# The same 1286 items of a gated delta-rule plus softplus MLP kernel, issued in another order

## The chip, the core and the metric

One core of one Trainium2 chip. The metric is device time in microseconds (us) of one execution; lower is better. Three runs of the kernel before took 242.27, 242.74 and 242.04 us: a median of 242.27.

The engines are named as the profile names them: PE (matrix multiply) with PEld (its weight loads), DVE (vector), ACT (scalar), POOL (GpSimd) and SP (the queue that issues most transfers). Each takes its own instructions strictly in order; between engines only semaphores order the work.

## What is computed

```python
# q, k, v, g: [4, 8, 768, 48]; beta: [4, 8, 768]; w_in: [384, 2048]; w_out: [2048, 384]
k_n = k / (np.linalg.norm(k, axis=-1, keepdims=True) + 1e-06)
state = zeros((B, H, D, D))
for t in range(S):
    y[:, :, t] = g[:, :, t] * (q[:, :, t] @ state)
    v_old = state^T @ k_n[:, :, t]
    state = state + beta[:, :, t] * outer(k_n[:, :, t], v[:, :, t] - v_old)
x = y.transpose(0, 2, 1, 3).reshape(3072, 384)
out = softplus(x @ w_in) @ w_out
```

The loop is written here in short form; sums run over the 48 features of a head.

## The kernel before, in words

The 768 steps are cut into 12 chunks of 64. The chunks are taken in six pairs (0 and 1, 2 and 3, and so on). All the work is recorded first, as 1286 items, each a small function that emits a few instructions and knows which items it depends on. Then `Program.emit` walks the words of the table `_ORDER`. A word is a letter and a number: `G281` emits item 281 on POOL; P is PE, D is DVE, A is ACT, S is SP. The table alone sets the order on every engine and, where an item may run on more than one engine, which one. It also sets which buffer an item gets: each ring of buffers gives the one that came free first at that place of the table, and an item waits until the last user of its buffer is done.

Some items matter below. The stages of a chunk c are:

- `load`: k, q, v and g come in two halves of 192 KB each, issued by SP (L302 for q, L305 for the others). Items 25 + 8c and 26 + 8c are k, the next two q, then v, then g. `bload` (17 to 24) are eight small transfers of beta.
- `ksq`, `red`, `sqrt` or `pow`, `eps`: the norms of k. A square (L351 on ACT, L353 on POOL), a sum on DVE (L362), a root (ACT for chunks 0 to 3, L373 on POOL after that), a reciprocal (L383).
- `kmul` (L406) scales k by its norm for chunks 2 and up; chunks 0 and 1 are only cast. `cast q` makes q 16-bit. `trs` are transposes on PE (L422 for k, L454 for q), `kev` and `qev` copy them out of PSUM.
- `gram` (L516): products of k and q within the chunk. `kkc` (L209 or L213) copies, `mask` (L498) masks them.
- For each pair, the inverse of a triangular matrix: `ln` (L597 or L604), `pick` (L627), `clear`, `diag`, two `prep` (L644), then 15 `step` items in a strict chain, step 0 with one instruction (L656) and each later one with a multiply (L664) and an add (L671), on DVE or POOL. Then `ca` and `cb` (L686, L688), the stream transposes `st` (L714), `tx`, and three small product stages per chunk: `xmm`/`xs`, `tmm`/`td2`, `zmm`/`z`. The items of the first pair are 225 to 272 (steps 231 to 245), of the second 313 to 360 (steps 319 to 333).
- The recurrence of the chunk: `ks` and `qs` (L826) multiply by the state, `vs` (L842) and `w` (L866; `w0`, L858, in chunk 0) form the right side, `umm` (L880), `u1`, `zu` (L893), `u2` solve, `smm` (L910) and `s` (L924) give the next state, `ymm` (L936) and `y` (L950) the output, `ytr` (L963) and `xt` transpose it for the MLP. Chunk c + 1 needs `s` of chunk c.
- The MLP: `g1` (L989) multiplies by w_in, `soft` (L1001) is the softplus on ACT, `g2` (L1016) multiplies by w_out, `o` copies the result, `store` (L1035) writes it. Chunks 0, 1, 10 and 11 go alone, with a moving size of 256 in `g1`; chunks 2 and 3, 4 and 5, 6 and 7, 8 and 9 go in pairs with 512, so `g1 2.*` and `g1 4.*` begin a pair. `wload` (121 to 128, L330) are the eight weight transfers, issued by POOL: 121 to 124 the quarters of w_in, which are called w0.0 to w0.3, and 125 to 128 those of w_out.
- `fill` (L1046): four matmuls on the identity whose result nobody reads. They are optional: the table may hold any number of them.

PSUM has eight banks: five for the small stages (ring `d`), two for `g1` (ring `h`), one for `g2` (ring `o`). SBUF has 12 buffers for loaded k, q, v, g and for the squares of k (ring `f`).

What sets the order is thus the table alone. SP's list is a queue with loads and stores in one line: a store at its head waits for its `o`, and all loads behind it wait too. POOL's list mixes arithmetic with the weight transfers.

## Time and profile before

| | |
|---|---|
| median of 3 runs | 242.27 us (242.04 to 242.74) |
| span of the profiled execution | 241.5 us |
| PE busy | 219.4 us, 91% |
| of it, `g1` and `g2` | 74.0 and 77.7 us |
| of it, `fill` (13 items, 52 matmuls) | 18.1 us |
| DVE, ACT, POOL busy | 161.7, 152.8, 113.7 us |
| loads and weights, HBM read | 25.26 MB |

The span runs from the first to the last instruction of the profiled execution. Its own time outside the profiler isn't listed; the median of the runs is 0.8 us above its span.

How to read it: times are from the span's start. A busy share is an average over stages that have different limits. An idle engine costs nothing unless the engine that sets the end waits for it. Starts and ends of PE's matmuls overlap, since they are pipelined, and the spans on POOL are rough.

### The profile page before, as it was taken

How to read it: one execution, taken by the hardware profiler on the slowest of the kernel's cores; microseconds unless marked ns; L12 is line 12 of the kernel's file. 1: busy time of each engine (PE TensorE's matmuls, PEld its weight loads, DVE VectorE, ACT ScalarE, POOL GpSimd, SP SyncE). 2: the span in 40 equal slices, each digit the busy share in tenths (PEclk: the TensorE clock that was granted, in tenths of full speed). 3: DMA queues.
4: the chain of work that ended last, by engine and by line, in shares of the span. 5: the costliest groups of instructions: out<-in, count | busy, mean ns of one | idle time of the engine just before them, and what ended most of it. 6: DMA issues, size and time to landing. Idle time of an engine off the chain costs nothing.

```text
span 241.5 us, 11396 instructions
## 1 busy us (share of the span) xinstructions
PE 219.4 (91%) x5020; PEld 135.6 (56%) x5020; DVE 161.7 (67%) x368; ACT 152.8 (63%) x292; POOL 113.7 (47%) x197
## 2 busy tenths in 40 slices
PE   7645877879988999999999999999999999999983
PEld 2423455646764664556655566655565555677751
DVE  2768699888897889987899757896496310623000
ACT  5767576764982778876895767757363674143540
POOL 8740393875779778989597482016620000000000
PEclk9985599999999999999999999999999999999999
DMA  6999989999999399961889514962302311303112
GB/s 102 182 245 137 167 135 190 176 173 180 180 217 167 57 177 164 162 113 35 150 153 184 97 30 94 160 122 52 69 21 52 68 34 25 64 19 81 35 33 65
DMA packets 86833, 27.57 MB, mean 114 GB/s; under 512 B 77048, under 2 KB 86776, under 8 KB 86784
## 3 DMA queue, kind: packets, MB, share of 16 engines
q1 hardware_dynamic: 80624, 20.83, 52.6%
q0 software_dynamic: 3840, 3.17, 8.5%
q10 hardware_dynamic: 2320, 2.85, 5.2%
q8 instruction: 39, 0.64, 1.2%
q14 instruction: 10, 0.08, 0.1%
HBM read 25.26 MB, written 4.72 MB: 124 GB/s over the span
## 4 chain that ended last, share of the span: by engine, by line
PE 75%; DMA 7%; DVE 6%; SPq 4%; issue 3%; ACT 2%; POOL 1%; DVEq 0%; ACTq 0%; POOLq 0%
PE o L1016 27%; PE h L989 26%; DMA w_in<-in_moe_w_in_dram 4%; PE d L826 3%; SPq L305 3%; PE d L936 3%; PE d L516 2%; DMA f<-in_q_dram 2%; PE d L422 2%; PE d L963 2%; PE d L454 2%; PE d L880 2%; PE d L910 2%; PE d L893 2%; PE d L768 1%
## 5 line engine op out<-in xcount | busy, mean ns | idle before, releaser
L1016 PE MATMUL o<-w_out,ga 128*128 128x384 f16 x384 | 77.7, 327 | 0.7 <-ACT osb L209 0.6
L1001 ACT ACTIVATE ga<-h 128x512 f16<-128x512 f32 x96 | 56.5, 599 | 29.8 <-PE h L989 25.9
L989 PE MATMUL h<-xt,w_in 128*128 128x512 f16 (+1 forms) x384 | 74.0, 327 | 0.5 <-DMA w_in<-in_moe_w_in_dram 0.3
L989 PEld LDWEIGHTS <-w_in 128*128 128x128 f16 x384 | 34.5, 98 | 21.2 <-DMA w_in<-in_moe_w_in_dram 0.8
L1016 PEld LDWEIGHTS <-ga 128*128 128x128 f16 x384 | 33.7, 98 | 21.8 <-issue 0.8
L664 POOL TENSOR_TENSOR tmp<-nn,tt 128x78 f32<-128x78 f32 (+7 forms) x53 | 19.2, 362 | 16.1 <-DVE tt L671 13.0
L373 POOL TENSOR_TENSOR nv<-nv,half_c 128x16 f32<-128x16 f32 x8 | 23.5, 2940 | 6.6 <-DVE nv L362 6.5
L671 POOL TENSOR_TENSOR tt<-tt,tmp 128x78 f32<-128x78 f32 (+7 forms) x53 | 20.4, 385 | 4.2
L498 DVE TENSOR_TENSOR mt<-d,mask 128x256 f16<-128x256 f32 x48 | 18.2, 413 | 4.5 <-PE d L516 3.5
L209 ACT ACTIVATE kqt<-d 128x1024 f16<-128x1024 f16 (+1 forms) x18 | 18.0, 1000 | 4.8 <-PE d L454 3.6
L211 DVE CAST u<-d 128x384 f16<-128x384 f32 x20 | 10.9, 554 | 14.3 <-PE d L880 7.9
L209 ACT ACTIVATE u<-d 128x384 f16<-128x384 f32 x28 | 13.0, 490 | 11.8 <-PE d L880 5.4
L1046 PE MATMUL h<-ident 128*128 128x512 f16 x52 | 18.1, 493 | 1.7 <-DVE ident L197 1.7
L209 ACT ACTIVATE kk<-d 128x256 f16<-128x256 f32 x37 | 13.4, 386 | 6.3 <-PE d L516 5.4
L209 ACT ACTIVATE osb<-o 128x384 f32<-128x384 f32 x19 | 9.3, 492 | 9.4 <-PE o L1016 9.3
L454 PE MATMUL d<-ident,qn 128*128 128x128 f16 x96 | 8.5, 243 | 6.7 <-ACT qn L209 5.9
L950 DVE TENSOR_TENSOR yg<-d,f 128x384 f16<-128x384 f32 x24 | 12.3, 551 | 2.9 <-PE d L936 2.8
L924 DVE TENSOR_TENSOR s<-s,d 128x384 f16<-128x384 f16 x20 | 10.4, 542 | 5.7 <-PE d L910 4.3
L644 POOL TENSOR_TENSOR nn<-ln,beta_l 128x256 f32<-128x256 f16 x8 | 6.1, 780 | 14.2 <-DVE ln L627 14.2
L209 ACT ACTIVATE xt<-d 128x768 f16<-128x768 f16 x10 | 8.1, 813 | 7.0 <-PE d L963 7.0
L866 DVE TENSOR_TENSOR w<-f,d 128x384 f16<-128x384 f32 x22 | 11.3, 545 | 1.4 <-ACT xt L209 0.7
L362 DVE TENSOR_REDUCE nv<-f 128x16 f32<-128x768 f32 x12 | 11.3, 942 | 1.0 <-ACT f L351 1.0
(117 smaller groups left out, 346.7 us busy)
## 6 DMA issues: line engine op xcount, KB each, us to landing
f<-in_k_dram SPq DMA_DIRECT2D x24, 192.0 KB, 5.7
f<-in_q_dram SPq DMA_DIRECT2D x24, 192.0 KB, 5.6
f<-in_v_dram SPq DMA_DIRECT2D x24, 192.0 KB, 5.3
f<-in_g_dram SPq DMA_DIRECT2D x24, 192.0 KB, 5.3
out_dram<-osb ACTq DMA_DIRECT2D x29, 96.0 KB, 2.7
out_dram<-osb SPq DMA_DIRECT2D x19, 96.0 KB, 2.8
w_in<-in_moe_w_in_dram POOLq DMA_DIRECT2D x4, 384.0 KB, 7.9
w_out<-in_moe_w_out_dram POOLq DMA_DIRECT2D x4, 384.0 KB, 8.4
```

The costliest lines, as they stand in the source:

```text
L209: nc.scalar.activation(o, x, AF.Copy, scale=float(sign))
L362: lambda en: nc.vector.tensor_reduce(nvs().rearrange("p (a h) -> p a h", a=2), ksq.ap, mybir.AxisListType.X, ALU.add),
L373: nc.gpsimd.tensor_tensor(nvs(), nvs(), half_c[:, :NU], ALU.pow)
L454: nc.tensor.transpose(o[:, j], qn.ap[:, j].rearrange("p m d -> p (m d)"), ident)
L498: nc.vector.tensor_tensor(mt[c][m].ap[:, NP * p : NP * p + NP], gb[m].ap.rearrange("p (i b) -> p i b", i=NP)[:, :, n : n + C], mask[:, Non ...
L664: ENG[en].tensor_tensor(t, nn.ap[:, :, j : j + 1, j + 1 :].broadcast_to([P, 2, w, n]), tt.ap[:, :, :w, j : j + 1].broadcast_to([P, 2, w, n ...
L671: ENG[en].tensor_tensor(rows, rows, t, ALU.add)
L950: lambda en, m=m: nc.vector.tensor_tensor(heads(yg.ap, m), hd(yp[m].ap), heads(gf.ap, m), ALU.mult),
L989: nc.tensor.matmul(hp.ap[:, n * b : n * b + n], w_in[:, j, f * P : (f + 1) * P], xt.ap[:, j, t0 : t0 + n], start=(j == 0), stop=(j == 2),)
L1001: lambda en, hp=hp, o=gb: nc.scalar.activation(o.ap, hp.ap, AF.Softplus),
L1016: nc.tensor.matmul(op.ap[:, :DM], b.ap[:, col + c0 : col + c0 + 128], w_out[:, f, :], start=(f == 0), stop=(f == NF - 1),)
L1046: nc.tensor.matmul(hp.ap, ident, ident[:, None, :].broadcast_to([P, 4, P]))
```

## The change

Only the text of `_ORDER` is changed. Items, dependences, ring sizes and shapes are the same. Counted over the two tables:

- SP's loads. Before: k0, k1, q2, v0, half of k3, q1, q0, q4, q3, the rest of k3, half of g0, k2, k4, ... After: k0, k1, q1, q0, half of k3, k2 and k3 mixed with one half of q2, half of g0, q3, q4, v0, k4, the other half of q2, the rest of g0, v1, g1, ... The eight `bload` go from places 19 to 33 of SP's list to places 10 to 28. SP issues 27 of the 48 stores (19 before), ACT 21 (29 before).
- The first inverse: steps 3, 4, 5, 8, 9, 11, 12, 13 and 14 run on POOL, the others on DVE. Before, step 2 ran on POOL, the others on DVE. All 15-step chains together: 68 steps on POOL (58 before), 22 on DVE (32 before).
- The second inverse: its two `prep` and step 10 move from POOL to DVE, steps 2, 3, 5, 6, 7, 9 and 12 from DVE to POOL, so that step 10 is the only one left on DVE.
- POOL's list up to the second inverse. After: cast k0 (half), five copies, clear, clear, diag, cast q0, the nine steps, w0.3, w0.0, kmul 2, ksq 4, diag, cast q2, the two `w0` of chunk 0 (items 714 and 715), w0.1, kmul 3, pow 4, w0.2, two quarters of w_out, vs 1, kmul 4, two quarters of w_out, then the steps. Before: copies, cast k1 (half), cast q2, `w0` twice, diag, step 2, ksq 2, tx, w0.0, w0.2, w0.1, clear, ksq 4, two of w_out, diag, pow 4, kmul 4, w0.3, vs 1, the two `prep`, steps.
- `kmul` 2 and 3 move from DVE to POOL; six of the 12 `xt` move from ACT to DVE; single `cast`, `kev`, `kkc`, `td2`, `u1`, `u2`, `z`, `o` move in both directions.
- PE: 10 `fill` items (13 before). In chunk 2, `smm` stands before `ymm`, and `ks` of chunk 3 stands before `ytr` of chunk 2; before, `ymm` stood before `smm` and `ytr` 2 before `ks` 3. On DVE, `w` of chunk 3 stands before `ln` of the third pair (item 401); before, it stood behind it.
- Before the first `g1` of the pair of chunks 2 and 3 (item 992 before, 1000 after) PE's list holds the same items in both tables, but for the fills and for the last `g2` of chunk 1, which stands behind it after.

The tables up to the first `g1` of the pair of chunks 2 and 3; the rest is permuted in the same manner:

```diff
@@ -1064,72 +1064,72 @@
 _ORDER = """
-S26 S25 P138 P161 S33 S34 P151 A12 G4 S44 A173 S43 G2 A169 D176 P177 P174 D0 G227 A178 P188 D170 A15
-A3 S29 G1 D175 P182 A189 A171 D204 S30 S49 A190 A197 D183 P205 D206 S36 G201 A11 P158 S35 S28 D184
-G9 D198 P202 G280 D203 D172 P281 A199 D200 D225 P216 G714 P210 A211 A212 G715 D226 P141 A282 P185
-A187 A7 S27 S60 S59 S52 D5 P213 A217 A10 A207 S51 S50 A218 A179 P180 A214 A181 A186 G228 D229 D230
-S22 P208 A209 D231 D232 G233 D234 D235 D236 P133 S32 S24 A215 S41 D237 D238 D239 D240 D241 D242 D243
-D244 D245 D248 D246 A293 D250 S23 S42 G273 A368 P369 S57 A370 S66 P145 P194 P136 P255 A247 A249 S31
-S58 S17 D196 P264 D251 D195 S18 D257 A254 D256 G253 P258 A300 G8 D252 G121 D265 A260 P301 P135 G123
-D294 S20 D266 S19 D274 G6 A259 P261 P716 A13 A295 A262 A263 A717 A718 P191 D192 A275 S21 P719 A720
-S38 S37 D193 D302 D721 P147 A713 G122 D16 P219 S65 G315 G14 G361 G126 P725 D221 G125 D220 P722 D727
-D726 G316 P728 D296 P137 D276 D297 D277 A724 A723 A729 P934 P928 A935 A929 D362 G363 P298 D299 P926
-A927 S40 P278 D279 P303 A304 P308 A310 A309 P930 D306 D305 P283 A284 A285 P936 D307 D312 D364 P288
-A931 D311 G365 D287 D292 P731 P932 A289 A290 A937 S39 D291 D286 D313 G124 P366 P267 A268 A269 G730
-P150 P270 S67 S45 A933 D314 G317 G318 D733 A381 G319 G320 A367 D732 S46 D382 P735 A737 A736 D272
-D271 P949 P950 D321 D322 G127 G323 P222 D224 P734 S68 D223 D324 D325 S73 P738 P938 A739 A740 P744
-A939 D326 D745 P940 G327 P371 P741 D746 D328 P747 G128 P164 S81 D742 A748 G329 A372 S99 D743 A941
-G330 P951 D374 P970 A373 D331 P376 A388 P956 A971 G332 D379 D380 P749 D375 S74 G333 A378 D334 P958
-A377 A957 D751 G383 A959 D336 P964 D338 A337 P389 S82 A335 P962 A390 D339 G342 P952 A965 S48 P343
-D384 P352 S76 A341 D345 D344 G385 A953 D750 D340 P960 P346 A449 A348 S84 P942 A961 S47 A963 D347
-D354 P753 A754 P349 A469 S75 P966 D450 D351 G451 A350 D755 D353 P968 S83 A967 P386 D470 S100 S98
-D387 P752 P756 D758 P943 D757 G471 S53 D452 P391 A393 S54 P944 D392 A954 D395 P762 D394 D764 P396
-A397 A955 P759 D760 A398 P945 D761 A946 D401 S97 P355 P972 G403 G453 A356 A969 P454 G476 S55 A357
-P973 D763 A455 S56 P765 D402 G404 G405 D400 P974 A766 D399 G406 P767 A456 P358 D769 P975 G407 A360
-D768 G408 P457 D359 A976 A978 S977 P770 G409 D458 G410 P771 A772 P979 S105 D773 A557 P477 D411 P774
-G412 D775 A776 S62 P980 A564 D472 P780 S61 G413 A478 P777 D781 P981 D782 G414 A947 D473 P783 A784
-P459 P982 D460 D461 P992 A983 D462 D778 P474 S64 A993 P1008 D558 S92 A475 P1000 D779 A1009 P464 S89
-D463 P479 A1001 P986 D468 A481 S113 D482 A466 D483 P990 D480 G415 G491 G416 G417 G418 G419 A987 D465
...
+A2 S25 S26 G173 G7 P132 A4 P160 D176 G9 A169 S34 S33 G12 D170 P155 G1 S35 S36 S27 S28 S49 S23 D5 D6
+D13 A14 A201 G8 D204 A197 P174 P177 D3 D175 D0 D198 P205 P202 A206 A203 P210 A171 D172 A199 A211
+A212 A15 D200 D178 P182 D225 G315 G227 P130 D183 D184 D226 G228 D229 G179 D16 D230 S42 S44 D231 D232
+D233 S18 S41 S21 S50 S32 S22 P180 A181 P194 A273 D207 S51 S60 S17 S19 S29 S52 S58 S20 S59 S24 D195
+D274 D196 G234 S30 P208 P185 A209 G235 A187 A186 P188 P213 A214 P216 A217 A215 P219 D10 G236 D237
+D238 G239 P154 G240 D241 G242 G243 G244 G245 A275 A11 D190 D221 A293 D294 D220 S57 S43 P191 D193
+D192 S31 S37 D276 D248 A368 A249 A189 S38 S39 D246 S40 P135 D250 A295 A247 D296 P166 A218 S65 S66
+G124 G121 G277 G361 G316 P255 G280 G714 P369 A370 A713 D251 P264 P278 D300 D257 D253 D254 D256 P258
+G715 P157 A259 D252 G122 G297 S46 S45 A260 P261 A263 D266 D362 D265 G363 P716 S74 S73 A717 P168 P281
+A262 D718 G123 A279 P719 A721 A720 P301 P298 D302 P725 A299 A282 D727 D726 P153 P303 A304 S68 S67
+D305 D306 P728 P288 D307 D291 D403 A729 A289 P308 P283 G126 G125 G730 D364 D311 D312 D292 A290 A309
+P928 P722 G365 A310 A284 A285 D287 S82 S81 P267 A929 A724 A268 P932 D313 D314 D317 D318 A933 P222
+P938 P940 A723 A269 A939 P731 P926 A941 A927 D224 D223 D286 P366 P270 D733 D732 P936 P735 S48 A272
+D271 P734 P934 S47 A937 A737 D736 P738 A740 P930 G127 D367 P371 A372 A931 G128 D739 P744 D745 G319
+G320 G321 D746 P949 G322 G323 G324 G325 G326 G327 G328 D329 G330 G331 P747 P950 P741 D742 D743 S53
+A748 P956 A935 A957 G332 G333 S54 P376 P962 D374 A963 D379 D378 D380 D375 P958 P951 G381 P966 D337
+A373 A334 A335 P952 D336 D338 D404 P749 P343 A959 A953 A967 A377 D339 P942 G341 D345 D382 S75 D750
+P964 P943 P970 A971 G342 S76 D344 D340 P346 P352 A348 D751 D353 P944 A347 P349 P753 A449 D354 A351
+G383 D350 D384 G385 A754 A755 D388 P960 D450 D579 P752 P756 P389 D757 A961 P945 A758 P759 D946 A390
+A469 P386 D760 D761 D470 P762 P968 S56 S84 S83 A387 P391 P972 S55 G451 D452 D763 G453 G456 P396 A969
+A965 A393 A392 P973 D394 D395 D400 D399 A398 A397 D764 P767 P355 A356 A357 D768 G471 D769 S98 S97
+P454 P974 P771 A455 P358 A773 P765 P975 A359 A360 A772 A766 A976 P770 P774 D401 D402 D405 D406 D407
+D408 D409 D410 A776 A775 P457 P979 P780 A476 P777 D781 D782 D778 D779 P980 A458 P477 P783 A478 D784
+A557 P981 P459 D472 D473 P1000 P1012 P474 A1001 D461 D462 D463 A1013 P1008 P992 P464 A475 P479 A1009
+A993 P990 G411 G412 G413 G414 D415 D416 D417 G418 G419 G420 G421 P986 D468 A460 A466 D482 D481 D483
...
 """
```

81 lines of the change are left out of this document (41 added, 40 removed).

## The prediction

> **What bounds the kernel now.** First the page, then the windows, then the engines' timelines.
>
> ```profile
> span 241.5 us, 11396 instructions
> PE 219.4 (91%) x5020; PEld 135.6 (56%) x5020; DVE 161.7 (67%) x368; ACT 152.8 (63%) x292; POOL 113.7 (47%) x197
> PEclk9985599999999999999999999999999999999999
> DMA  6999989999999399961889514962302311303112
> ...
> L1046 PE MATMUL h<-ident 128*128 128x512 f16 x52 | 18.1, 493 | 1.7 <-DVE ident L197 1.7
> ```
>
> ```profile
> 0.00:18.00 18.00, 11.21 (x236) 5.79 (x236) 10.31 (x36) 11.62 (x25) 11.99 (x27) 0.97 1.04 176
> 18.00:30.00 12.00, 8.71 (x72) 4.42 (x76) 9.35 (x28) 8.03 (x13) 1.82 (x2) 0.50 1.09 155
> 0.00:90.00 90.00, 72.57 (x1846) 47.12 (x1847) 72.40 (x177) 60.18 (x118) 58.34 (x92) 0.92 1.03 166
> 90.00:238.00 148.00, 146.80 (x3176) 88.52 (x3174) 89.29 (x192) 92.54 (x175) 55.38 (x105) 1.00 0.47 84
> ```
>
> The columns after the length are PE, PEld, DVE, ACT, POOL, clock, DMA share, GB/s. Behind 90 us PE is busy 146.8 of 148 us: it sets the end there. Ahead of 90 us it is busy 72.57 us, of which 18.1 are fills, so 90 - 72.57 + 18.1 = 35.5 us bring the result no nearer. Only there can an order win much. What ends that part is the first 512-wide `g1`, which needs `xt` of chunk 3:
>
> ```profile
> 40.51 0.72 PE L989 MATMUL h<-xt,w_in 128*128 128x256 f16 x5 [0.34 <-DMA w_in<-in_moe_w_in_dram]
> ...
> 89.77 0.81 PE L989 MATMUL h<-xt,w_in 128*128 128x512 f16 x3
> ```
>
> The first row is the very first `g1`; the second is where the saturated part begins. From there to the end of the span it is 241.5 - 89.8 = 151.7 us, and PE has the same items left in both orders (one `g2` more in the new one, 0.7 us). So the sum is: the new time of that matmul, plus 151.7 + 0.7 = 152.4. The median is 0.8 us above the span, which I add at the end.
>
> Four marks lie on the way there: the first inverse's end, chunk 0's output, the second inverse, and the recurrence of chunks 2 and 3.
>
> **The loads.** In the first 18 us the transfers run at 176 GB/s (first window), so a half of 192 KB takes 1.1 us of the 16 engines, and the digits show them full until slice 13.
>
> ```profile
> 26.91 1.47 POOL L353 TENSOR_TENSOR f<-f 128x768 f32<-128x768 f32 x1 [9.52 <-DMA f<-in_k_dram]
> ...
> 31.69 8.77 DMA w_in<-in_moe_w_in_dram
> ```
>
> The first row is POOL's timeline: `ksq` 2 waits 9.5 us for k2, whose last half is the 21st load. In the new order it is the 12th: 9 x 1.1 = 10 us earlier, about 17 to 18 us; k3 follows at 19. The price is on the other side: v0 goes from the 8th to the 21st place, 13 x 1.1 + 5 more beta transfers, so it lands near 28 us instead of 13; the second half of q2 becomes the 23rd (near 32), k4 the 22nd (near 30).
>
> **The first inverse.** Nine steps go from DVE to POOL, one comes back.
>
> ```profile
> L671 POOL TENSOR_TENSOR tt<-tt,tmp 128x110 f32<-128x110 f32 x3 | 1.2, 407 | 0.2
> L664 POOL TENSOR_TENSOR tmp<-nn,tt 128x110 f32<-128x110 f32 x3 | 1.2, 393 | 0.7 <-DVE tt L671 0.6
> L671 DVE TENSOR_TENSOR tt<-tt,tmp 128x110 f32<-128x110 f32 x3 | 0.8, 273 | 0.1
> L664 DVE TENSOR_TENSOR tmp<-nn,tt 128x110 f32<-128x110 f32 x3 | 0.8, 271 | 0.1
> L362 DVE TENSOR_REDUCE nv<-f 128x16 f32<-128x768 f32 x7 | 6.6, 945 | 0.2 <-ACT f L351 0.2
> ...
> 16.29 0.22 DVE L671 TENSOR_TENSOR tt<-tt,tmp 128x56 f32<-128x56 f32 x1
> ...
> 16.65 0.32 POOL L664 TENSOR_TENSOR tmp<-nn,tt 128x78 f32<-128x78 f32 x1 [1.95 <-DVE tt L671]
> ```
>
> A step of this width is 0.80 us on POOL and 0.54 on DVE: 0.26 more, and a POOL instruction leaves a slightly longer gap (last column: 0.2 us before three, against 0.1). The nine are 30 to 126 wide; I take 0.28 for each, 2.5. A handover costs 0.14 (16.29 + 0.22 to 16.65), and there are five against two: 0.5. DVE is to do `red` 2 (0.95) and two masks between steps 2 and 6, of which some 0.5 us stick out beyond POOL's three steps; step 2, which returns, gives 0.3 back. Together +3.2. What the chain starts from stays where it was, since its inputs k0 and k1 are still loaded first.
>
> ```profile
> 24.59 0.78 DVE L688 TENSOR_SCALAR ta<-tt,mx 128x256 f16<-128x256 f32 x2
> ...
> 47.48 1.93 DVE L604 STREAM_TRANSPOSE ln<-kk 128x1024 uint32<-128x1024 uint32 x1
> ...
> 62.74 0.44 DVE L688 TENSOR_SCALAR ta<-tt,mx 128x256 f16<-128x256 f32 x1 [0.25 <-POOL tt L671]
> ...
> 78.05 1.96 DVE L604 STREAM_TRANSPOSE ln<-kk 128x1024 uint32<-128x1024 uint32 x1
> ```
>
> On DVE's timeline the first row is where the first inverse's result is taken; it moves from 24.6 to 27.8 us. The Trainium skill, GPSIMD Engine Reference, section 4.1, speaks against such a move: two-input elementwise work is to stay on VectorE, about 2x slower on GpSimd. The rows above say 1.5x; by the page the nine steps would cost some 5 us, and the result would be 242.5.
>
> **Chunk 0.** Behind the steps POOL has two weight issues (0.8 each), `kmul` 2, `ksq` 4, a diag, `cast q` 2 and both `w0`. The rows:
>
> ```profile
> L353 POOL TENSOR_TENSOR f<-f 128x768 f32<-128x768 f32 x3 | 4.4, 1468 | 9.5 <-DMA f<-in_k_dram 9.5
> L858 POOL TENSOR_TENSOR w<-f,nv 128x384 f16<-128x384 f32 x2 | 1.6, 834 | 1.3 <-DVE bl L582 1.3
> 46.07 1.47 POOL L406 TENSOR_TENSOR kn<-f,nv 128x768 f16<-128x768 f32 x1 [0.73 <-DVE nv L383]
> 33.67 0.44 PE L880 MATMUL d<-w,td 64*64 64x48 f16 x32 [0.25 <-DVE xs L753]
> ```
>
> 27.8 + 1.6 + 1.5 + 1.5 + 0.2 + 0.8 + 1.7 = 35.1, if k4 and q2 have landed by 31 and 32.6, which is just in time. So `umm` 0 starts at 35.4 instead of 33.7, and the first `g1` at about 42 instead of 40.5. This is not yet a loss of 1.5 us: PE has no lack of `g1` of chunks 0 and 1 to do later, while it waits for chunks 2 and 3.
>
> **The second inverse.** `kmul` 3 on POOL comes at 35.1 + 0.8 (w0.1) + 1.5 = 37.4, so the transposes of k3 at 38, four us ahead of before, and `ln` 2 about 43.3 instead of 47.5. But POOL has more in line: `pow` 4, three weight issues, `vs` 1, `kmul` 4, two weight issues.
>
> ```profile
> L373 POOL TENSOR_TENSOR nv<-nv,half_c 128x16 f32<-128x16 f32 x5 | 14.7, 2934 | 6.0 <-DVE nv L362 5.9
> 48.38 1.49 POOL L842 TENSOR_TENSOR f<-f,nv 128x768 f32<-128x768 f32 x1
> 51.75 0.24 POOL L656 TENSOR_TENSOR tt<-nn,tt 128x30 f32<-128x30 f32 x1
> ```
>
> 37.4 + 3.3 (with its add) + 5 x 0.8 + 1.5 + 1.5 = 47.7 for step 0, against 51.75. Seven steps more run on POOL and one fewer: 7 x 0.26 less 0.2 for the two that change places, so 12.6 us in place of 11.0. It ends at 60.3, 2.4 us ahead of 62.7.
>
> **Chunks 2 and 3.** From the inverse's end to the first 512-wide `g1` it takes 89.8 - 62.7 = 27.0 us before. Where it is lost:
>
> ```profile
> 69.06 0.44 PE L880 MATMUL d<-w,td 64*64 64x48 f16 x32 [0.50 <-DVE td L211]
> 73.02 0.35 PE L893 MATMUL d<-u,z 64*64 64x48 f16 x21 [0.76 <-issue]
> 76.49 0.43 PE L910 MATMUL d<-u,kn 64*64 64x48 f16 x31 [0.40 <-DVE yg L950]
> 80.51 0.51 PE L963 MATMUL d<-ident,yg 128*128 128x128 f16 x6
> 81.60 0.44 PE L826 MATMUL d<-s,kqt 48*64 48x48 f16 x32
> ```
>
> `ks` 3 starts at 81.60. Its state needs only `smm` 2 and `s` 2 (1.0 us), but on PE it stands behind `ytr` 2 at 80.51, and that waits for a `y` which DVE does behind `ln` of the third pair (1.96 us from 78.05). The new table puts `ks` 3 ahead of `ytr`, `smm` 2 ahead of `ymm`, and `w` 3 ahead of `ln`. By rows, `umm` 2 to `smm` 2 needs two `u` copies, `zu`, two more copies: 3 to 4.5 us in place of 7.4; `smm` 2 to `ks` 3 has 4.1 us of PE items in place of 5.1. Against it stand `ln` 4, `pick`, two `prep` and four steps on DVE (some 5 us) between `w` 3 and `y` 3, which the solve of chunk 3 (5 us on ACT and PE) about covers, and `xt` 3 behind both `s` on DVE, 1.0. Item by item I get 25 us from inverse to `g1`; since before shows unexplained waits such as the 0.76 above, I add 1.5: 26.5.
>
> 60.3 + 26.5 = 86.8, 3.0 ahead of 89.8. Plus 152.4: span 239.2, time 240.0. Behind 90 us POOL is busy 55.4 of 148 us and DVE 89.3; the moves shift some 8 us onto POOL over the run, and the cover is that slack; were it gone, those 8 us would come on top. Three fewer fills are costed at nothing, being idle time's work.
>
> **The rivals.**
>
> *The late loads hold POOL (slower).* POOL is in order: if k4, q2 or v0 land 6 us later than I count, because w0.3 and w0.0 (8.8 us for one in the chain above) share the same engines from 28 us on, then `w0`, `kmul` 3, `vs` 1 and step 0 of the second inverse all move by 6, to 53.7. For: the DMA share is over 1 in that stretch. Against: v0, q2 and k4 are issued by then. It decides from step 0 at 50.0, where 50.0 + 12.6 + 26.5 + 152.4 = 241.5, the span of before. At 53.7 it is 3.7 us more: 246.0.
>
> *The lead is given back (same).* Behind 90 us the recurrence of chunks 4 and 5 must come as much earlier too. One place speaks against it: SP's new list has the second half of v5 behind a store of chunk 2, which waits for that chunk's last `g2`. Then PE idles some 2.3 us near 105: 242.3.
>
> *The clock (same).* The granted clock is 0.50 from 18 to 30 us and back behind. If fewer fills leave it there until 42 us, the three fills and six transposes on chunk 0's path take 4 us more, half of which reaches the second inverse through POOL: 242.0. The Trainium skill, TensorE: Matmul & The Clock Gate, Part 1, has this rule: a busy window of about 3.4 us releases the clock, an idle one of that length takes it back. The 12 us row agrees in kind.
>
> *The full lead.* Without the 1.5 us that I added, and with `ks` 2 a further microsecond earlier: 237.5.
>
> **How the numbers follow.** Forecast 240.0 with 0.42; late loads 0.30; given back 0.11; clock 0.06; full lead 0.11. No change means within 0.3%, or 0.7 us, of 242.3, about what a measurement of this kernel can tell. Faster: 0.42 + 0.11 + some of the clock's and of partial returns, 0.56; same 0.13; slower 0.31. The likeliest case alone spans 238.3 to 241.5 (1.5 us of small waits either way); the range of 237.0 to 246.0 takes in both ends of the unknown landings.
>
> **What would show it.** Right: k2's square before 20 us; the first inverse's result near 27.8; the first `g1` near 42, yet the second `ca` near 60; `ks` 3 before 78; the first 512-wide `g1` near 87; PE full from there. Wrong: POOL idle for a transfer between 28 and 45, step 0 of the second inverse behind 50.0, or PE idle behind 90 us.

## The result, and the profile after

The kernel after took 260.62 us (median of 258.56 to 261.35), against 242.5 for the kernel before in the same comparison: ratio 1.071, interval 1.063 to 1.078. Slower by 7% where 1% faster was forecast. Some executions of these kernels are a few per cent longer at a lower granted clock; the medians here count them, the ratios leave them out. The profiled execution took 259.99 us with a span of 258.3, 16.8 above the span of before.

The page of after; rows as before:

```profile
span 258.3 us, 11364 instructions
PE 227.7 (88%) x5008; PEld 141.5 (55%) x5008; DVE 168.8 (65%) x361; ACT 148.0 (57%) x284; POOL 121.2 (47%) x212
PEclk9755555867999799999999999999999999999999
DMA  7997999999907505991969921793010023003113
...
L1046 PE MATMUL h<-ident 128*128 128x512 f16 x40 | 17.3, 599 | 1.7 <-DVE ident L197 1.7
```

PE is busy 8.3 us more and idle 8.5 us more (30.6 in place of 22.1). Of the fills there are ten in place of 13, yet they take nearly as long: 599 ns each in place of 493, as more of them run at the halved clock (slices 3 to 7 show a 5, before two did).

DVE's timeline of after at the end of the first inverse, then POOL's over the same time:

```profile
27.67 7.19 DVE L688 TENSOR_SCALAR ta<-tt,mx 128x256 f16<-128x256 f32 x2 [0.35 <-POOL tt L671]
34.90 1.05 DVE L714 STREAM_TRANSPOSE dn<-ta 128x512 uint32<-128x512 uint32 x1
```

```profile
27.57 1.63 POOL L330 DMA_DIRECT2D w_in<-in_moe_w_in_dram  x2
29.23 1.49 POOL L406 TENSOR_TENSOR kn<-f,nv 128x768 f16<-128x768 f32 x1
30.67 1.47 POOL L353 TENSOR_TENSOR f<-f 128x768 f32<-128x768 f32 x1
32.08 0.23 POOL L637 COPY tt<-beta_l 128x32 f32<-128x32 f32 x1
32.23 0.82 POOL L211 CAST qn<-f 128x768 f16<-128x768 f32 x1
33.02 1.61 POOL L858 TENSOR_TENSOR w<-f,nv 128x384 f16<-128x384 f32 x2
34.58 0.80 POOL L330 DMA_DIRECT2D w_in<-in_moe_w_in_dram  x1
36.36 1.47 POOL L406 TENSOR_TENSOR kn<-f,nv 128x768 f16<-128x768 f32 x1 [0.98 <-DVE nv L383]
```

The two `ca` scalings, 0.78 us together before, take 7.19. The first is done by 28.1; the second (item 246) begins at 28.03 and ends at 34.86. POOL in the meantime works off its train (instructions that follow each other without a pause) from 27.57 on; both `w0` are done at 34.6, w0.1 is issued by 35.4. An instruction like item 246 is called held in what follows: it has begun, waits for no semaphore, and ends only when POOL's work beside it has ended. So the rule of the first section, that only semaphores order the work between engines, has an exception here. PE gets the result only then, its clock at a half:

```profile
36.00 0.62 PE L744 MATMUL d<-dn,kk 64*64 64x32 f16 x32 [6.89 <-DVE nv L381]
```

```profile
30.00:42.00 12.00, 5.43 (x116) 3.57 (x115) 11.44 (x14) 3.17 (x5) 7.01 (x9) 0.50 1.34 179
102.00:258.00 156.00, 147.82 (x3178) 89.76 (x3176) 95.18 (x201) 89.89 (x170) 55.30 (x105) 1.00 0.45 84
```

The second fence is of windows (PE, PEld, DVE, ACT, POOL, clock, DMA share, GB/s). DVE seems full there (11.44 of 12 us); most of that is one held instruction. The chain that ended last names the hold, and three pieces later on in which PE waited for nothing:

```profile
27.67 7.20 DVE ta L688 x2
...
67.20 0.85 issue
...
82.44 1.85 issue
...
126.74 1.20 issue
```

The marks of the prediction, read from both traces (us; starts, where no end is named; the last line is from the first 512-wide `g1` to the last item's end):

```
                          before   after   predicted
first inverse's result     24.6    27.67   27.8
umm 0                      33.67   43.17   35.4
first g1                   40.5    52.8    42
end of kmul 3              40.24   37.83   37.4
step 0, second inverse     51.75   58.80   47.7
its end                    62.7    71.61   60.3
ks 3                       81.60   91.14   under 78
first 512-wide g1          89.77  101.37   86.8
the rest                  148.8   154.0    149.5
```

The loss of 16.8 is 11.6 ahead of the first 512-wide `g1` and 5.2 behind it.

### The profile page after: what moved, and what is told of

Its sections match the earlier page's. It is cut to its first block, busy times and chain, and to the rows that moved or that the text cites. A ratio compares the mean times of both kernels' runs of the same rounds, so it can differ in the third digit from the quotient of the medians.

```text
span 258.3 us, 11364 instructions
## 1 busy us (share of the span) xinstructions
PE 227.7 (88%) x5008; PEld 141.5 (55%) x5008; DVE 168.8 (65%) x361; ACT 148.0 (57%) x284; POOL 121.2 (47%) x212
## 2 busy tenths in 40 slices
DMA packets 86833, 27.57 MB, mean 107 GB/s; under 512 B 77048, under 2 KB 86776, under 8 KB 86784
## 4 chain that ended last, share of the span: by engine, by line
PE 61%; DVE 16%; POOL 7%; ACT 6%; issue 5%; DMA 3%; SPq 0%; ACTq 0%; POOLq 0%; DVEq 0%
PE o L1016 20%; PE h L989 20%; POOL tmp L664 3%; POOL tt L671 3%; DVE ta L688 3%; PE d L936 3%; DVE mt L498 3%; PE d L454 2%; PE d L826 2%; PE d L422 2%; PE h L1046 2%; ACT kk L209 2%; PE d L768 2%; DMA f<-in_k_dram 2%; PE d L893 2%
## 5 line engine op out<-in xcount | busy, mean ns | idle before, releaser
L989 PE MATMUL h<-xt,w_in 128*128 128x512 f16 (+1 forms) x384 | 75.6, 334 | 0.4 <-ACT ga L1001 0.3
L989 PEld LDWEIGHTS <-w_in 128*128 128x128 f16 x384 | 35.8, 100 | 22.6 <-issue 1.1
L664 POOL TENSOR_TENSOR tmp<-nn,tt 128x126 f32<-128x126 f32 (+7 forms) x65 | 24.3, 373 | 19.7 <-DVE tt L671 15.3
L209 ACT ACTIVATE kqt<-d 128x1024 f16<-128x1024 f16 (+1 forms) x21 | 20.5, 985 | 17.4 <-PE d L454 14.3
L671 POOL TENSOR_TENSOR tt<-tt,tmp 128x126 f32<-128x126 f32 (+7 forms) x65 | 25.0, 384 | 5.1
L1046 PE MATMUL h<-ident 128*128 128x512 f16 x40 | 17.3, 599 | 1.7 <-DVE ident L197 1.7
L406 POOL TENSOR_TENSOR kn<-f,nv 128x768 f16<-128x768 f32 x8 | 11.9, 1490 | 10.5 <-PE d L910 7.1
L209 ACT ACTIVATE osb<-o 128x384 f32<-128x384 f32 x17 | 8.4, 494 | 14.2 <-PE o L1016 14.1
L516 PE MATMUL d<-kqt 48*64 48x128 f16 (+1 forms) x448 | 12.3, 226 | 3.6 <-ACT kk L209 1.2
L516 PEld LDWEIGHTS <-kqt 48*64 48x64 f16 x448 | 8.4, 117 | 11.1 <-issue 10.6
L866 DVE TENSOR_TENSOR w<-f,d 128x384 f16<-128x384 f32 x22 | 11.6, 544 | 2.7 <-ACT ga L1001 1.7
```

Source lines behind the costliest of these rows:

```text
L209: nc.scalar.activation(o, x, AF.Copy, scale=float(sign))
L516: nc.tensor.matmul(gb[m].ap.rearrange("p (i b) -> p i b", i=NP)[HALF[r], i, lo:hi], x[:, :C], x[:, lo:hi],)
L664: ENG[en].tensor_tensor(t, nn.ap[:, :, j : j + 1, j + 1 :].broadcast_to([P, 2, w, n]), tt.ap[:, :, :w, j : j + 1].broadcast_to([P, 2, w, n ...
L671: ENG[en].tensor_tensor(rows, rows, t, ALU.add)
L989: nc.tensor.matmul(hp.ap[:, n * b : n * b + n], w_in[:, j, f * P : (f + 1) * P], xt.ap[:, j, t0 : t0 + n], start=(j == 0), stop=(j == 2),)
L1046: nc.tensor.matmul(hp.ap, ident, ident[:, None, :].broadcast_to([P, 4, P]))
```

## The experiments

In the expectations the tables are spoken of as front, middle and rear: up to the first inverse's products, from there to the first 512-wide `g1`, and behind it. Of the tables' lines only the words around an edit are shown. In an edit that moves words, the places that they leave are not shown.

### What holds VectorE

Item 246 on ACT:

```diff
-S38 S39 D246 S40 P135
+S38 S39 A246 S40 P135
```

> The changed kernel with one word of the table altered: `ca` 0.0 on ACT instead of DVE; everything else, POOL's train of six instructions at 29.2 to 34.6 us included, stays. Theory (DVE's `ca` 0.0 cannot run while POOL runs back to back, and the 6.4 us it waits are what chunk 0, POOL's later list and the second inverse lose): `ca` 0.0 takes about 0.4 us, the first `xmm` starts near 30 instead of 36.0, step 0 of the second inverse comes at 49 to 53 instead of 58.8, the first 512-wide `g1` at 91 to 95 instead of 101.4, the time falls by 6 to 10 us to 250 to 254 us. Rival 1 (the longer POOL list itself, nine steps and the late loads, is what costs): `ca` may be short, but step 0 stays behind 56 and the time at 257 or more. Rival 2 (the low clock of 12 to 48 us is a cause by itself, not a result): the clock stays at 0.50 to 48 us and the time falls by less than 4 us.

258.69 us, ratio 1.064 (1.055 to 1.072). On ACT it took 0.71 us, but then DVE's timeline shows a scaling of 128 x 16 held in its place, an `eps` that takes 0.13 us elsewhere:

```profile
30.09 4.37 DVE L381 TENSOR_SCALAR nv<-nv 128x16 f32<-128x16 f32 x1
```

So it is no property of `ca`: the next DVE scaling is held instead, until POOL's train ends (both `w0` are done at 34.42 there).

Two one-column memsets (items `gap`) behind each of seven of the train's items:

```diff
+    def gap(en):
+        nc.gpsimd.memset(spare, 0.0)
+        nc.gpsimd.memset(spare, 0.0)
...
-G124 G121 G277 G361 G316
+G124 G1286 G121 G1287 G277 G1288 G361 G1289 G316 G1290
```

> The changed kernel with seven breaks in POOL's list, one behind each of two weight issues, `kmul` 2, `ksq` 4, the diag, `cast q` 2 and `w0` 0: two one-column memsets of the same tile, so that the second waits for the first and POOL stands still for some 0.1 us; everything else stays. What is known by now: with `ca` 0.0 on ACT the next DVE scaling, `eps` 3, was held for 4.37 us until POOL's train ended, and in the probe kernel, whose POOL instructions stood 0.08 us apart because each waited for the one before, a DVE instruction was held for one POOL instruction only, whatever the train's length. Theory (a train whose instructions follow without a gap holds DVE until its end; a gap of 0.08 us lets DVE in): no DVE instruction in 27 to 37 us takes more than 2.0 us; the first `xmm` starts at 30 to 32.5 instead of 36.0, `umm` 0 at 36.5 to 39 instead of 43.2, step 0 of the second inverse at 50 to 54 instead of 58.8, the first 512-wide `g1` at 92 to 97 instead of 101.4, the time is 250 to 256 us. Rival 1 (the gaps do nothing, DVE is held by the lock for the length of POOL's work in any case): a DVE instruction of over 4 us in that stretch, time 258 or more. Rival 2 (the hold is gone but is not what costs): no long DVE instruction, time 258 or more.

254.86 us, ratio 1.048 (1.043 to 1.053). POOL's train takes longer (both `w0` are done at 36.7, 2.1 us later), and the kernel is faster: DVE's timeline of it (its code lies one line further down) has no single instruction over 1.41 us in that stretch; the second row is two copies.

```profile
27.63 0.82 DVE L689 TENSOR_SCALAR ta<-tt,mx 128x256 f16<-128x256 f32 x2 [0.34 <-POOL tt L672]
...
31.97 1.71 DVE L212 COPY tx<-tb 64x512 f16<-64x512 f16 x2
```

The first 512-wide `g1` comes at 97.58, 3.8 us earlier: that is the price of the hold, less what the longer train costs. Next, only the two weight issues at the train's head moved, with no memset:

```diff
-G124 G121 G277 G361 G316 P255 G280 G714
+G277 G361 G316 P255 G280 G714
...
-G715 P157
+G715 G124 G121 P157
```

> The changed kernel with two words of POOL's list moved: the weight issues w0.3 and w0.0 stand behind the train (`kmul` 2, `ksq` 4, diag, `cast q` 2, both `w0`) instead of in front of it. No instruction is added. What is known: with breaks of some 0.1 us in the train the hold was gone; in the probe kernels a DVE scaling beside POOL's products was held for one product at a time, even without a gap between them, except where weight issues stood ahead of two products, where one scaling was held for 5.08 us, through both. Theory 1 (a weight issue ahead makes POOL keep what DVE needs until POOL next stands still): no DVE instruction in 26 to 37 us over 1.9 us, several held for one POOL instruction each; `xmm` 0 at 29 to 32 instead of 36.0, time 252 to 256.5 us. Theory 2 (a train without gaps is enough): one instruction held for 4 to 6 us as before, time 257 or more.

256.93 us, ratio 1.057 (1.046 to 1.067). The first 512-wide `g1` comes at 98.69, 2.7 us earlier. The same POOL products now hold each DVE instruction for one product at the most:

```profile
27.77 1.96 DVE L688 TENSOR_SCALAR ta<-tt,mx 128x256 f16<-128x256 f32 x2 [0.33 <-POOL tt L671]
...
30.72 0.67 DVE L381 TENSOR_SCALAR nv<-nv 128x16 f32<-128x16 f32 x1
```

POOL pauses 0.74 us behind its first product there, so the first row alone wouldn't tell; the `eps` of the second row is held by a product that the next POOL instruction follows without a pause, and is let go at its end.

The nine steps alone put back on the engines of before:

```diff
-D233 G234 G235 G236 G239 G240 G242 G243 G244 G245
+G233 D234 D235 D236 D239 D240 D242 D243 D244 D245
```

> The changed kernel with the steps of the first inverse on the engines of the kernel before (step 2 on POOL, the other 14 on DVE); all else of the new order stays. Theory: the hold depends on where POOL's train falls. The inverse's result comes near 25 to 26 us (27.7 before this edit), while POOL's train, which needs the norm of k2 from DVE, cannot start before 25 to 27; so the two `ca` may escape it, but one of DVE's scalings or casts behind them meets it; I expect one hold of 3 to 6 us and a time of 250 to 259 us. Rival 1 (the nine steps on POOL are by themselves what costs, as the forecast's +3.2 us): the time falls by 3 to 4 us, no more, whatever DVE's instructions show. Rival 2 (the loads or the chunk-2 order cost it): no change, 258 or more, without a hold.

261.01 us; the four runs lie between 256.24 and 262.94, too far apart to tell a gain or a loss. In the profiled one (260.63 us) the first 512-wide `g1` stands at 102.34, no earlier than in after. The inverse ended at 27.32, only 0.3 earlier, since DVE then does the steps and its masks and sums one behind the other. The weight issues stand more than 10 us ahead of the train there, and no DVE instruction is held for more than one product (a `ca` of 1.65 us). But `ca` begins only at 30.1, and `umm` 0 at 42.11.

Four probes, one run each, measured the hold by itself; all leave the computation out. In each case POOL runs a train while DVE runs 2 to 14 instructions, mostly scalings (0.4 us alone). The first three vary the train's length, its gaps and the kinds of instruction; the fourth, whose cases are shown, puts one weight issue ahead.

```diff
+    def free(n):
+        return [lambda po, i=i: G.tensor_tensor(px[:, i], fa, fb, ALU.mult) for i in range(n)]
...
+    case(0, free(4), [ca] * 8)
+    case(1, [dma(0)] + free(4), [ca] * 8)
+    case(2, [dma(1)] + free(1), [ca] * 8)
+    case(3, [dma(2)] + free(2), [ca] * 8)
+    case(4, [dma(3)] + free(6), [ca] * 8)
```

> A kernel that leaves the whole computation out and writes zeros to the first 128 rows only: 18 small cases one after the other, in each of which a few instructions of DVE run beside a train of n back-to-back instructions of POOL that share no data with them. Theory (a DVE instruction of this kind waits until POOL's whole train has ended): with trains of 1, 2, 4 and 6 products of 768 columns (1.47 us each) one `ca`-like scaling (0.43 us alone) is stretched to about 1.5, 3, 6 and 9 us, and 2 of them in a case are never both stretched. Rival 1 (it waits for one POOL instruction at most): never above 1.47 + 0.43 = 1.9 us, whatever n. Rival 2 (POOL has nothing to do with it): 0.4 us in every case. By the Trainium skill, SBUF - State Buffer, section Who interferes with whom, scalings and copies in a two-port mode and products of two SBUF tensors wait, while reductions, a PSUM source and ACT do not; so I expect cases 8 stretched, 9, 10 and 11 not.

> The probe kernel again (the computation left out, zeros written to 128 rows), 17 cases, now with trains on POOL whose instructions write different tiles, so that none waits for another and they follow without a gap; only case 12 keeps the train that waits for itself. Theory: the DVE instruction that is caught is held until the train's end, so with trains of 1, 2, 3, 4 and 6 products (1.8 us each here) it takes about 1.9, 3.7, 5.5, 7.3 and 11 us; in the case with six products and eight `ca` one single `ca` is long and the others take 0.43; products of two SBUF tensors on DVE are held in the same way; a PSUM source and ACT are not. In case 12 each caught `ca` takes 1.86 us again. Rival (one POOL instruction at most, the gap does not matter): 1.86 us in all cases.

> The probe kernel with trains that really have no gap: POOL's products write six parts of one tile, none waits for another (in the probe before, where they wrote six tiles, the trace still showed 0.08 us between them and each caught instruction held for one product, 1.86 us). The computation is left out, zeros go to 128 rows. Theory: where POOL's instructions follow without a gap (each starting before the one ahead has ended), the caught scaling is held to the train's end: about 1.9, 3.6, 5.4, 7.2 and 10.8 us with 1, 2, 3, 4 and 6 products; with eight `ca` beside six products only one is long. Rival (one POOL instruction at most): 1.86 us each, several in a row.

> The probe kernel, 11 cases (the computation left out, zeros to 128 rows). In each, DVE has eight or more scalings of 0.43 us beside POOL products of 1.8 us that follow without a gap; in some a weight issue stands ahead of them on POOL. Theory 1 (the weight issue ahead makes the difference): with none (cases 0 and 5) each caught scaling is held for one product, 1.9 us, several in a row; with one issue ahead of 1, 2, 4 and 6 products (cases 2, 3, 1, 4) one scaling is held to the train's end, about 2.5, 4.3, 8 and 11.5 us; with two waiting memsets or a pause of 3 us between the issue and the products (cases 6 and 7) it is one product again; products of two SBUF tensors on DVE are held in the same way (case 8), scalings from PSUM not at all (case 9); with the issue in the middle of the train (case 10) the first holds are of one product, the last goes to the end. Theory 2 (the issue is no cause): 1.9 us at most in all cases but those that showed it by chance.

The first three: beside 768-column products each held scaling of `ca`'s kind took 1.86 to 2.06 us, about one product, whatever the train's length, so POOL and DVE take turns. Each of them had a case with two weight issues ahead of two products that broke the pattern. In the first two probes the products of this case stood 0.08 us apart; one scaling of 3.20 and 3.33 us lasted to the end of the first product, and the next took 1.86. In the third, without a pause, one of 5.08 us lasted through both products. The last probe followed that up. The longest scaling of each case (start, end, us), with a weight issue ahead of 1, 2, 4 and 6 products, then six products without one:

```
 25.093  27.514   2.421   issue + 1
 31.480  35.661   4.181   issue + 2
 13.315  21.124   7.809   issue + 4
 39.626  50.816  11.190   issue + 6
 54.319  56.374   2.055   no issue, 6
```

and on POOL, for the case with four:

```profile
12.86 0.93 POOL L97 DMA_DIRECT2D w_in<-in_moe_w_in_dram  x1
13.81 7.07 POOL L127 TENSOR_TENSOR px<-fa,fb 128x768 f16<-128x768 f32 x4
20.85 0.46 POOL L76 TENSOR_TENSOR po<-fa,fb 128x64 f16<-128x64 f32 x1
```

The scaling ends at 21.12, the fourth product at 20.88. With the two memsets between issue and products, or a pause of some 3 us, it was 1.86 again; a scaling from PSUM wasn't held (0.48); a product of two SBUF operands was (7.75).

Two runs that were to make the same thing in the kernel before missed:

```diff
+        for _ in range(6):
+            ENG[en].tensor_tensor(scr.rearrange("p (a b) -> p a b", b=32), hb, hb, ALU.mult)
```

> The kernel before with one item added: when the last step of the first inverse is done (24.5 us), POOL runs a useless train, one small copy and six products of 512 columns (about 1.0 us each, 6 us in all); `ca` 0.0 and 0.1 stay on DVE. Theory: the second of the two `ca`, 0.4 us before, lasts until the train's end, 5 to 6 us, and the kernel takes 4 to 7 us more than the same kernel with both `ca` on ACT. Rival (it waits for one instruction of POOL at most): 1.0 us more in the `ca`, and the two kernels are within 1.5 us of each other.

> The kernel before with the same useless train on POOL at the end of the first inverse, and both `ca` of the first pair on ACT. Theory: no `ca` is stretched (0.4 us each); what is left is the train's own price on POOL, 0 to 5 us over the kernel before (242 to 247 us). Rival: as slow as the kernel with `ca` on DVE, within 1.5 us.

The useless train started at 17.5, beside the steps and not beside `ca`, so 252.25 and 254.23 us say nothing on `ca`. They do show the instructions of DVE's steps at 1.06 to 1.10 us in place of 0.29 while it ran: held one POOL product at a time, without a weight issue.

The Trainium skill, SBUF — State Buffer, section "Who interferes with whom", says that a DVE instruction in a two-port mode or with two SBUF inputs and a GpSimd instruction share a port pair under an exclusive lock: the first one has it "for the whole instruction", and the other blocks fully. The rows without an issue agree (1.86 for one product, 0.48 from PSUM). With a weight issue ahead they don't: DVE waits for the whole train (11.19 for six products).

### Front, middle, rear

Three kernels join the two tables: the words of one up to a place, then what is left in the order of the other (written in short; the kernels hold the joined tables).

```diff
-_ORDER = before
+_ORDER = before[:496] + rest_of(after)    # h1_rear
...
+_ORDER = before[:221] + rest_of(after)    # h2_late
...
+_ORDER = after[:213] + rest_of(before)    # h3_front
```

> A table put together from both: the first 496 words of the table before (up to the first 512-wide `g1`), and behind them what is left, in the order and on the engines of the changed table. Theory: the part behind the first 512-wide `g1`, which took 156.9 us in the changed kernel and 151.7 in the one before, costs its 4 to 5 us by itself (PE idle about 4 us, one `g2` more), whatever stands ahead of it: first 512-wide `g1` near 90, time 246 to 248.5 us. Rival (that part was slow only because its loads and chunks came in late and crowded): 241.5 to 244 us.

> The first 221 words of the table before (up to the output and state of chunk 0, some 44 us), then what is left in the order and on the engines of the changed table; fills of the changed table that belong to the first part are left out. Theory (the first 45 us of the new order, with DVE held and `smm` 0 late, bring the whole 11.6 us at the first 512-wide `g1`): no DVE instruction held for over 2 us, step 0 of the second inverse at 52 or before, the first 512-wide `g1` at 87 to 92, and with the rear's own 4 to 5 us a time of 242 to 248 us. Rival (the middle part, the second inverse and chunks 2 and 3 in the new order, costs much of it too): first 512-wide `g1` behind 95, time over 251 us.

> The reverse: the first 213 words of the changed table (new loads, first inverse on POOL, POOL's train, chunk 0 up to `ymm` 0 and the first grams of chunk 3), then what is left in the order and on the engines of the kernel before, so that `smm` 0 comes at once. Theory: the hold of DVE is there (an instruction of 4 to 7 us in 27 to 36 us), the first `xmm` near 36, `smm` 0 within 7 us behind `umm` 0 (10.9 in the changed kernel); the middle and rear parts are the old ones, so the time is the old one plus what the front loses by the hold and the low clock: 249 to 254 us. Rival (the front by itself costs little, the middle or rear is at fault): under 246 us.

249.32 us (ratio 1.026, 1.019 to 1.033), 254.65 (1.044, 1.036 to 1.053) and 253.13 (1.040, 1.033 to 1.047). The rear and the front lose by themselves. With the front and middle of before, the first 512-wide `g1` stands at 89.77 to the hundredth and what follows takes 154.9 in place of 148.8. With the rear of before, it takes 148.4 behind a `g1` at 100.46, and the hold is there (6.83). The second kernel has a mishap of its own, the first `g1` behind the joint waiting 3.4 us for w0.3, which the joint left late; with that issue moved:

```diff
-G122
+G122 G124
```

> As the table with 221 words of the kernel before ahead of the rest in the new order (254.65 us), with the weight issue w0.3 moved into the first part, since there `g1` 0.12, first in the new order of PE, waited for its late landing until 52.4 us and held `ks` 1 behind it. Theory (that wait was made by joining the two tables; the new middle part by itself costs 1 to 3 us): `ks` 1 at 50 to 53 instead of 55.1, the first 512-wide `g1` at 90 to 93 instead of 95.2, and with the new rear's 6 us a time of 248.5 to 252 us. Rival (the new middle part costs its 5 us in any case): first 512-wide `g1` at 94 or later, 253 us or more.

253.68 us, ratio 1.037 (1.025 to 1.050); first 512-wide `g1` at 94.16, as the expectation's rival had it. So behind the front of before the middle costs 4.4 us, in the marks and in the medians (253.68 against 249.32 for the rear alone); the four runs lie 3.9 us apart, so this is rough. Behind the front of after it costs less: 101.37 against 100.46, 0.9 us. The parts don't add up, and what is put down to each depends on the one ahead of it.

Two edits test single claims on the middle. `smm` 0, the product that `kmul` 4's square buffer waits for, moved ahead, on top of the memsets:

```diff
-P725
+P722 A724 A723 P725
```

> The changed kernel with the seven breaks in POOL's train (254.9 us) and one more edit: `smm` 0 stands on PE ahead of `ymm` 0 and the grams of chunks 2 and 3, with both `s` 0 behind it, as in the kernel before; with the breaks alone it came 11.1 us behind `umm` 0 (3.8 in the kernel before), and `kmul` 4 on POOL waited 3.3 us for the buffer that it frees. Theory (that wait holds POOL's list and the recurrence of chunk 1): `smm` 0 at 42 to 44 instead of 48.8, `kmul` 4 at 46 to 47 instead of 49.6, `ks` 1 earlier than 55.3, the first 512-wide `g1` 1 to 4 us earlier than 97.6, time 251 to 254 us. Rival (the second inverse waits for `ln` 2 from DVE at 50.2, and PE's clock of 0.50 sets that, so that `smm` 0 gains nothing): step 0 stays at 53 to 54, the first 512-wide `g1` within 0.7 us of 97.6.

252.81 us, ratio 1.040 (1.030 to 1.050). `smm` 0 came at 42.2 in place of 48.8 and `kmul` 4 at 47.6 in place of 49.6, but step 0 at 53.57 (53.46) and the first 512-wide `g1` at 97.29 (97.58): the second inverse didn't wait for `kmul` 4 any more but for `ln` 2 and the two `prep` on DVE. So it went as the expectation's rival said, but not for the clock: that was 1.0 from 42 to 57 us there (0.75 in the memset kernel), and step 0 gained nothing by it. The median time is 2.0 us below the memset kernel's, but the intervals of the ratios overlap.

And the recurrence's new order alone, in the kernel before:

```diff
-P391
+P759 D760 D761 P391
...
-D401
+P767 D769 D768 D401
```

> The kernel before with one part of the change alone: in chunk 2 `smm` 2 and both `s` 2 stand ahead of `ymm` 2, `ks` 3 ahead of `tmm` 3 and `ytr` 2, and both `w` 3 ahead of `ln` of the third pair. The forecast's own step: from the second inverse's end to the first 512-wide `g1` 25 to 26.5 us instead of 27.0, `ks` 3 before 78 instead of 81.6, and if PE is full from there on, a time 0.5 to 2 us below the kernel before. Rival (the stretch is bounded by PE's own items or by the solve of chunk 3, so that the order gains nothing): `ks` 3 earlier, but the first 512-wide `g1` within 0.5 us of 89.8 and the time within 0.3% of the kernel before.

246.66 us against 243.5, ratio 1.007 (1.002 to 1.012). `ks` 3 is earlier, 79.82, but 1.6 of these 1.8 us are there at `ks` 2 (60.48 in place of 62.05), ahead of the edit: from one to the other it takes 19.3 us (19.5). The first 512-wide `g1` is later, 92.84. PE's list shows why: `tmm` 3, `ytr` 2, transposes of k6 and three `g2` now stand behind `ks` 3, and `umm` 3 comes 7.0 us behind it (2.2 in before). There is a further reason, a stall inside a row of matmuls that read what the ones before them read; in before the stall at this place is 0.76:

```profile
70.21 0.26 PE L893 MATMUL d<-u,z 64*64 64x48 f16 x11
72.29 0.35 PE L893 MATMUL d<-u,z 64*64 64x48 f16 x21 [1.82 <-issue]
```

### PE's instructions

Such stalls wait for no semaphore that the profile shows. Each ends 1.2 to 1.8 us behind the end of a 16 KB transfer on the queue called instruction. A span has 39 such transfers for the 10040 matmuls and weight loads of PE in before, so each brings some 256 instructions. And every such stall over 0.2 us, in all kernels here and in the probe below, stands at the same kind of place: with PE's matmuls counted through, it comes ahead of number 96 plus a multiple of 128, to within one record (736 and 1376 in before; 992, 1376, 2400 and 2528 in after). As 128 matmuls and their weight loads are 256 instructions, these places are called seams here. Summed over a span the stalls are 1.3 us in before, 4.9 in after, 4.7 with after's rear alone, none with before's rear behind after's front, and 8.4 in the join with after's middle and rear, whose PE timeline has the longest:

```profile
56.15 0.63 PE L936 MATMUL d<-u,mt 64*64 64x48 f16 x29
60.00 0.21 PE L936 MATMUL d<-u,mt 64*64 64x48 f16 x3 [3.22 <-issue]
```

A probe with matmuls that depend on nothing, the computation left out:

```diff
+    pause(4)
+    small(0, 2048)
...
+    for i in range(12):
+        nc.sync.dma_start(out=load[i], in_=flat[128 * i:128 * i + 128, :768])
+    small(1, 2048)
+    take(1)
+    pause(16)
+    wide(2, 64)
```

> A probe of its own: the computation is left out. TensorE has, in this order: 2048 small matmuls (64x64 weights, 48 columns, each with its own weight load, so 4096 instructions) with no transfer going; the same 2048 while twelve loads of 393 KB run; 64 matmuls of 512 columns; 256 small ones. No matmul inside a train waits for another engine. In the kernels small matmuls take some 14 ns each (32 in 0.44 us), which is 256 instructions in 1.8 us; the transfers on the queue named instruction bring 256 instructions each, take 0.9 to 1.7 us, and the stalls of TensorE without any wait end 1.45 us behind the end of one. Theory (the rear and the middle lose time because TensorE's instructions arrive late behind bursts of small matmuls): in both small trains TensorE stands still again and again without waiting for anything, with each stall's end 1.2 to 1.8 us behind the end of a 16 KB instruction transfer; with loads beside it the transfers take longer, 1.2 to 2 us, and the second train is longer than the first; none in the 512-wide train, where 256 instructions last some 27 us. Rival (the stalls belong to some dependence of the kernels that the profile does not show): both small trains run without a gap over 0.15 us, 2048 x 14 ns = 28 us each.

Stalls there are, so the rival falls, but fewer and shorter than the theory had it. Eleven stalls, 7.6 us in 4352 small matmuls, at 11 of their 34 seams, each 1.21 to 1.56 us behind the end of such a transfer, and none among the 512-wide ones. At 13 more seams PE idles 0.12 us. PE's timeline at the start and from the second train, then windows:

```profile
5.06 6.12 PE L60 MATMUL ps<-x,w 64*64 64x48 f16 x223 [5.06 <-DVE x L54]
13.10 3.61 PE L60 MATMUL ps<-x,w 64*64 64x48 f16 x128 [1.92 <-issue]
17.11 3.08 PE L60 MATMUL ps<-x,w 64*64 64x48 f16 x109 [0.39 <-issue]
...
82.58 2.21 PE L60 MATMUL ps<-x,w 64*64 64x48 f16 x128 [0.51 <-issue]
86.03 3.13 PE L60 MATMUL ps<-x,w 64*64 64x48 f16 x128 [1.25 <-issue]
90.03 7.34 PE L60 MATMUL ps<-x,w 64*64 64x48 f16 x256 [0.88 <-issue]
```

```profile
4.00:12.00 8.00, 6.12 (x223) 6.04 (x223) 0.94 (x3) 0.00 (x0) 1.00 1.02 367
20.00:62.00 42.00, 41.05 (x1482) 40.08 (x1480) 0.00 (x0) 0.00 (x0) 1.00 0.02 5
90.00:136.00 46.00, 40.44 (x1441) 39.32 (x1441) 2.86 (x7) 0.00 (x0) 0.50 0.02 4
```

(PE, PEld, DVE, POOL; then clock, DMA share, GB/s.) The loads, issued behind nothing, ran from the start and not beside the second train: the DMA share is 1.02 up to 12 us, and there stands the longest stall, 1.92. With the transfers free a stall was 0.39 to 1.25 us, and for 42 us of the first train there was none over 0.12 us; the second train, with free transfers, has eight. So what makes one seam stall and another not is open, and so is why a stall in the kernels is as long as 3.22.

## Why the prediction was wrong, step by step

- *Right.* k2's square began at 17.3 (before 20 was said) and the first inverse's result is at 27.67 (27.8), for a chain that began 0.17 later: 2.9 us longer, where 3.2 was summed. Its terms weren't measured one by one. POOL's train took what was summed (both `w0` done at 34.6, 35.1 was said) and waited for no transfer. The second inverse is 12.8 us long from step 0 to its end (12.6).
- *The step that failed: "Chunk 0".* POOL's train was summed as plain time behind the steps, 35.1, and DVE's `ca` at 27.8 was taken to be free beside it, a term put at nothing. The train costs what was said; but its head of two weight issues keeps DVE out until it ends: item 246 takes 6.83 us. `umm` 0 isn't at 35.4 but at 43.17. Two edits that take the hold away in different ways show its price: the first 512-wide `g1` at 97.58 and 98.69 instead of 101.37, 3.8 and 2.7 us.
- *The rest of the front*, 3.4 us (97.58 without the hold, against 94.16 with the front of before), is in the main the DVE list. Without the hold `xmm` 0 is at 29.61, as early as in before (29.73), but `umm` 0 at 37.64 in place of 33.67. Of these 4.0 us more, 3.1 lie between `xmm` 0 and `tmm` 0 (4.6 in place of 1.5), where DVE now has a cast (0.94) and both `tx` (1.71) to do; the sum counted POOL alone on this path. With the weight issues moved, both `w0` are done at 34.2 and `umm` 0 still comes at 38.60, so POOL doesn't set it there. Part of the rest is PE's: the four fills ahead of `zmm` 0 take 1.89 us at a granted clock of 0.50 (1.03 at 1.00 in before). That these items cause it is read from the timelines; no run moved them alone.
- *"The second inverse"* forecast step 0 at 47.7 by POOL's list alone, with `ln` 2 on DVE done long before (43.3). It is at 58.8, and even with `smm` 0 early and no hold at 53.6. POOL's timeline of after, then DVE's:

```profile
41.84 2.94 POOL L373 TENSOR_TENSOR nv<-nv,half_c 128x16 f32<-128x16 f32 x1 [4.01 <-DVE nv L362]
...
55.08 1.47 POOL L406 TENSOR_TENSOR kn<-f,nv 128x768 f16<-128x768 f32 x1 [5.97 <-PE d L910]
56.50 1.55 POOL L330 DMA_DIRECT2D w_out<-in_moe_w_out_dram  x2
58.80 0.23 POOL L656 TENSOR_TENSOR tt<-nn,tt 128x30 f32<-128x30 f32 x1 [0.76 <-DVE nn L644]
```

```profile
55.17 0.42 DVE L498 TENSOR_TENSOR mt<-d,mask 128x256 f16<-128x256 f32 x1 [1.61 <-ACT kk L209]
55.52 1.93 DVE L604 STREAM_TRANSPOSE ln<-kk 128x1024 uint32<-128x1024 uint32 x1
57.48 0.45 DVE L627 COPY_PREDICATED ln<-mx,ln 128x256 uint32<-128x256 uint32 x1
57.96 0.76 DVE L644 TENSOR_TENSOR nn<-ln,beta_l 128x256 f32<-128x256 f16 x2
```

  POOL waits twice where the sum had no wait: `pow` 4 waits 4.01 us for DVE's sum of k4, and `kmul` 4 5.97 us for `smm` 0, which must be done with the buffer. But what ends last is DVE's list: `ln` 2 begins at 55.52, 12.2 us later than forecast, and step 0 waits for the two `prep` behind it. Without the wait for `smm` 0 it is the same list that ends last.
- *"Chunks 2 and 3"*, 26.5 from the inverse's end to the 512-wide `g1`, took 29.8. After does gain from `ks` 2 to `ks` 3 (16.2 in place of 19.5, with a stall of 1.85 us among it) and gives it back around it: the second `ca` stands 1.8 us behind the inverse's end on DVE, after an `s` of chunk 1, masks and a `kkc` that are late now, and from `ks` 3 to the `g1` it is 10.2 us (8.2). The run with the reorder alone gained nothing from `ks` 2 to `ks` 3 and made the kernel before 0.7% slower.
- *The rear*, forecast at 0.7 above the 151.7, is 5.2 above. Windows of before and of after, each beginning at the first 512-wide `g1`:

```profile
89.80:139.80 50.00, 49.86 (x1197) 28.36 (x1195) 43.53 (x97) 39.06 (x74) 39.04 (x67) 1.00 0.81 130
```

```profile
101.40:151.40 50.00, 46.69 (x1125) 27.17 (x1122) 43.45 (x96) 37.21 (x74) 31.12 (x46) 1.00 0.88 151
```

  PE is idle 3.3 of the first 50 us, where it was idle 0.1. Over the whole rear 3.8 of the 5.2 are idle time and 1.4 busy time, the one `g2` of 0.7 among it. "PE full from there" was taken from the windows of before for any order, and it is the order of the rear that leaves PE idle: the join with before's rear loses nothing there. Of the idle time 2.2 us are the stalls at seams (1.70 and 0.48). But the memset kernel idles 1.06 us at the place of the 1.70 (24.9 us behind the `g1`), there for ACT's `z`, and its rear takes 153.4 us with only 0.2 of such stalls. So the supply of instructions, to which the place and the time of these stalls point, is a real cost, but not shown to be the rear's cause: no run changed it, and how it shares the 3.3 us with late inputs stays open. The rival "given back" had a wait for v5 in this place, and no load is waited for.
- *"The late loads hold POOL"* was the rival on the right side, and its 246 was too small by 14.6. Its mechanism fell: POOL never waited for a transfer there.
- *"The clock"* was low as the rival had it: 0.50 from 30 to 42 us, beside a PE that was busy 5.43 of these 12. With the weight issues moved it is still 0.50 from 27.5 to 38.7 us, and the first 512-wide `g1` 2.7 us earlier: so much is the hold's without the clock. What the low clock adds in the front stays open; in the middle a full clock gained step 0 nothing.
- *A slip in the sums*: 1.5 us either way of 240.0 is 238.5 to 241.5, not 238.3. Nothing hangs on it.
